# Attention and maxout FFN on one core: score matmuls of two pairs of heads gathered into three half-array stretches per turn, with raw inputs in four buffers

## The chip, the cores and the metric

One Trainium2 chip; the kernel runs on one core of it. The metric is the device time in microseconds (us) of one execution. The kernel before takes 367.87 us (median of three runs). TensorE is called PE here, as in the profile (its weight loads PEld), VectorE DVE, ScalarE ACT, GpSimd POOL, and SyncE, which issues most transfers, SP.

## The reference

Softmax attention with a one added to the denominator, over 8 batches of 12 heads, 448 positions and 64 features a head, and behind it a feed-forward layer with three up projections, their maximum, and one down projection:

```python
def _attn_ref(q, k, v):                       # each 8 x 12 x 448 x 64
    scores = scale * np.matmul(q, k.transpose(0, 1, 3, 2))
    m = np.max(scores, axis=-1, keepdims=True)
    e = np.exp(scores - m)
    attn = e / (np.sum(e, axis=-1, keepdims=True) + np.exp(-m) + 1e-09)
    return np.matmul(attn, v).astype(np.float32)
...
x = np.ascontiguousarray(attn_out.transpose(0, 2, 1, 3)).reshape(B * S, H * D)
def _moe_ref(x, w1, w2, w3, w_out):           # 3584 x 768, weights 768 x 768
    h = np.maximum(np.maximum(x @ w1, x @ w2), x @ w3)
    return (h @ w_out).astype(np.float32)
```

The kernel leaves the maximum out, so its softmax is exp(s) / (1 + sum of exp(s)), which is the same number.

## The kernel before

**Pairs.** Two heads make a pair, six pairs a batch, 48 pairs in all. The 448 keys of a head are three blocks of 128 and one of 64; the last blocks of both heads of a pair are put into one block of 128, the "last rows".

**Attention of a pair.** `scores(p, c)` (L239) computes block c for both heads: two matmuls that contract over 64 features, one on the upper and one on the lower 64 rows of the array. These run side by side, and such a pair of matmuls is called a half-array pair here. `scores_last(p)` (L255) is one full matmul for the last rows. ACT takes the exponents from PSUM into `eT` (`exp_scores`, L249, both heads in one instruction of 896 elements) and `eL` (`exp_last`, L265). `av_main(p, hh)` (L273) multiplies them with v in three full matmuls for a head; v has columns of ones beside it, so that the sums of the exponents come out on the other 64 partitions. `av_last(p)` (L285) adds the last rows: one half-array pair. `reciprocals` (L298, L299) makes 1 / (1 + sum) by a logarithm for each head and one exponent on ACT. `normalize(p, hh)` (L307) multiplies on DVE and writes half of `xT` for one pair.

**Feed-forward.** When a batch's six pairs are normalized, `batch_done` puts 18 up groups (six matmuls over 448 tokens each, L356, closed by a DVE instruction, L370 or L372) and 6 or 8 output groups (six matmuls over 384 columns, L390, closed by L415, and two output transfers for every second one, L429) on a Python list. `group()` takes the next one from it. So the order on every engine is written out by hand: between the steps of one pair's attention stand groups of the batch before.

**The loop.** One turn of the loop (L452) handles pair `it` and finishes pair `it - 1`. From batch 2 on (`it` of 12 and up, `P_DMA`) a turn is: `cast_qk(it + 2)` on DVE, `transposes(it + 2)` as one transposing transfer on SP (L209), `scale_v(it + 1)` on POOL (L157); scores 0 and 1 with their exponents; a group; `av_main` of the pair before; `av_last` of the pair before, scores 2, `scores_last`; the reciprocals and the other exponents on ACT; a group; normalize head 0; a group; normalize head 1; the remaining one or two groups; the loads of pair `it + 5` (six transfers on SP). There are thus two places a turn where the array works in halves: scores 0 and 1 (two half-array pairs), and `av_last` with scores 2 (two half-array pairs). In batches 0 and 1 the transposes are done by PE. Batch 0 has no feed-forward work yet, and idle matmuls (`keep_busy`) stand in its place.

**Buffers.** Scores lie in two PSUM buffers (`ps_s`), attention results in two (`ps_av`), groups in two (`ps_u`). The transposed q and k have three buffers (`qkT`), the scaled v three (`vst`), the casts two (`qk16`). Raw q, k and v lie in three sets of buffers of three pairs each (`NRAW`, `HB`). When a turn begins a batch, four groups of the batch before last are still on the list (`LEFT`).

Of the kernel before, what the change touches and what calls it, by code (L numbers as in the profile page):

```python
# [10 lines left out]
FP32 = mybir.dt.float32  # L11
# [10 lines left out]
def kernel(  # L22
# [11 lines left out]
    nc = tc.nc  # L34
# [29 lines left out]
    small = ctx.enter_context(tc.tile_pool(name="small", bufs=2))  # L64
    xt_pool = ctx.enter_context(tc.tile_pool(name="xt", bufs=2))
    ht_pool = ctx.enter_context(tc.tile_pool(name="ht", bufs=2))
    out_pool = ctx.enter_context(tc.tile_pool(name="outp", bufs=3))

    ps_s = ctx.enter_context(tc.tile_pool(name="ps_s", bufs=2, space=bass.MemoryType.PSUM))
    ps_av = ctx.enter_context(tc.tile_pool(name="ps_av", bufs=2, space=bass.MemoryType.PSUM))  # L70
# [2 lines left out]
    ctx.enter_context(tc.manual_schedule())  # L73


    NRAW = 3
    HB = NPAIR // 2
    raw = [
        [cpool.tile([128, 2 * HB, NB + 1, D], FP32, name=f"{n}in{i}") for n in "qkv"]
        for i in range(NRAW)  # L80
# [2 lines left out]
    def load(p0, n_pairs, names="qkv", engs=(nc.sync, nc.sync)):  # L83
        b, j = divmod(p0, NPAIR)
        tiles = raw[(p0 // HB) % NRAW]
        h0 = 2 * (p0 % HB)
        for name, t, src in zip("qkv", tiles, (q, k, v)):
            if name not in names:
                continue
            rows = src[b, 2 * j : 2 * (j + n_pairs)].rearrange("h (p c) d -> p h c d", c=TP)  # L90
            hs = slice(h0, h0 + 2 * n_pairs)
            engs[0].dma_start(out=t[0:64, hs, 0 : NB + 1, :], in_=rows[:, :, 0 : NB + 1, :])
            engs[1].dma_start(out=t[64:128, hs, 0:NB, :], in_=rows[:, :, NB + 1 : TP, :])
# [5 lines left out]
    load(1, 1, "qk")  # L99
    load(0, 1, "v")  # L100
    load(2, 1, "qk")
    load(1, 2, "v")
    load(3, 1, "qk")
    load(4, 2, "q")
    load(3, 1, "v")
    load(4, 2, "k")
    load(4, 2, "v")

    idle = cpool.tile([128, S], MMDT, name="idle")
    nc.vector.memset(idle, 0.0)  # L110
    for i in range(NRAW - 1):
        nc.vector.memset(raw[i][0][64:128, :, NB, :], 0.0)
    nc.vector.memset(raw[2][0][64:128, 0:2, NB, :], 0.0)
    load(NPAIR, 1, "qk")

    ident16 = cpool.tile([128, 128], MMDT, name="ident16")
# [44 lines left out]
    def casts(p):  # L161
        cast_qk(p)
        scale_v(p)

    def cast_qk(p):
        qt, kt, _ = raw[(p // HB) % NRAW]
        h0 = 2 * (p % HB)
        hs = slice(h0, h0 + 2)
        k6, q6 = k16[p % NK], q16[p % NK]
        if p == 0:  # L170

            nc.scalar.copy(out=k6[:, 0:NB], in_=kt[:, hs, 0:NB].rearrange("p h c d -> p c h d"))
            for eng, cs in ((nc.scalar.copy, slice(0, 2)), (nc.vector.tensor_copy, slice(2, NB + 1))):
                eng(out=q6[:, cs], in_=qt[:, hs, cs].rearrange("p h c d -> p c h d"))
        else:
            if p >= P_DMA and (p // NPAIR) % 2:

                nc.vector.tensor_copy(
                    out=q6[:, 1 : NB + 1], in_=qt[:, hs, 0:NB].rearrange("p h c d -> p c h d")
                )  # L180
                nc.vector.tensor_copy(out=q6[64:128, 0], in_=qt[0:64, hs, NB])
            else:
                nc.vector.tensor_copy(out=q6, in_=qt[:, hs].rearrange("p h c d -> p c h d"))  # L183
            nc.vector.tensor_copy(  # L184
                out=k6[:, 0:NB], in_=kt[:, hs, 0:NB].rearrange("p h c d -> p c h d")
            )
        for hh, half in enumerate(halves):
            last = nc.gpsimd if p == 0 else nc.vector
            last.tensor_copy(out=k6[half, NB, hh], in_=kt[0:64, h0 + hh, NB])  # L189

    def scale_v(p):
        vt = raw[(p // HB) % NRAW][2]
# [58 lines left out]
    def scores_last(p):  # L251

        stl = ps_s.tile([128, 2, 512], FP32, tag="s", name="stl")
        qkT, q0, k0 = qkTs.pop(p)
        nc.tensor.matmul(  # L255
            out=stl[:, 0, 0:S],
            lhsT=qkT[:, k0 + NB * 128 : k0 + NB * 128 + 128],
            rhs=qkT[:, q0 : q0 + S],
            start=True,
            stop=True,  # L260
        )
        return stl

    def exp_last(p, stl):
        nc.scalar.activation(out=eL[:, p % 2], in_=stl[:, 0, 0:S], func=AF.Exp, scale=scale)  # L265
# [183 lines left out]
    casts(0)  # L449
    transposes(0)  # L450
    keep_busy(3)
    for it in range(NP + 1):  # L452
        p = it if it < NP else None
        prev = it - 1 if it > 0 else None
        to_next = NPAIR - it % NPAIR
        n_groups = -(-max(len(queue) - LEFT, 0) // to_next) if it % NPAIR else 4
        n_groups = max(3, min(5, n_groups))

        first = {3: 1, 4: 2}.get(it)
        if first is not None:  # L460
            hs = slice(2 * first, 2 * first + 2)
            nc.vector.memset(raw[2][0][64:128, hs, NB - 1 : NB + 1, :], 0.0)
            if first == 1:
                load(NPAIR, 1, "v")
            load(NPAIR + first, 1)
        if it in (3, 4):
            load_weight(0, it - 3)
        if it in (5, 6, 8):
            load_weight((5, 6, 8).index(it) + 1)
        if it < NPAIR:  # L470

            casts(it + 1)
            for c in range(2):
                exp_scores(p, c, scores(p, c))
            if prev is None:
                keep_busy(3)
                exp_scores(p, 2, scores(p, 2))
                transposes(1)
                exp_last(p, scores_last(p))
            else:  # L480
                den, av = (ps_av.tile([128, 512], FP32, tag="av", name=n) for n in ("den", "av"))
                sums_main(prev, den, 1)
                stp = scores(p, 2)
                sums_main(prev, av, 0)
                stl = scores_last(p)
                sums_last(prev, den, 1)
                sums_last(prev, av, 0)
                exp_scores(p, 2, stp)
                exp_last(p, stl)
                rb = reciprocals_one(den)  # L490
                transposes(it + 1)
            if it < NPAIR - 1:
                keep_busy(3)
            else:

                ups = [up_open()]
                up_part(ups[0], 0, 0, 0, range(3))
                av5 = ps_s.tile([128, 2, 512], FP32, tag="s", name="av5")
                sums_main(p, av5[:, 1], 1)
                sums_main(p, av5[:, 0], 0)  # L500
                sums_last(p, av5[:, 1], 1)
                sums_last(p, av5[:, 0], 0)
                rb5 = reciprocals_one(av5[:, 1])
            if prev is not None:
                normalize_one(prev, av, rb)
            if it == NPAIR - 1:
                normalize_one(p, av5[:, 0], rb5)
                batch_done(0)
        elif it == NPAIR:
            exp_scores(p, 0, scores(p, 0))  # L510

            up_part(ups[0], 0, 0, 0, (3,))
            ups.append(up_open())
# [12 lines left out]
            exp_scores(p, 2, scores(p, 2))  # L526
            exp_last(p, scores_last(p))
            group()
            transposes(it + 1)
            group()  # L530
        else:
            late = it + 1 < P_DMA
            if not late:

                if it + 2 < NP:
                    cast_qk(it + 2)
                    transposes(it + 2)
                if it + 1 < NP:
                    scale_v(it + 1)
            if p is not None:  # L540
                for c in range(2):
                    exp_scores(p, c, scores(p, c))
            group()
            if late:
                casts(it + 1)
            avs = [av_main(prev, hh) for hh in range(2)]
            av_last(prev, avs)
            if p is not None:
                stp = scores(p, 2)
                stl = scores_last(p)  # L550
            rb = reciprocals(prev, avs)
            if p is not None:
                exp_scores(p, 2, stp)
                exp_last(p, stl)
            if late:
                transposes(it + 1)
            group()
            normalize(prev, 0, avs, rb)
            group()
            normalize(prev, 1, avs, rb)  # L560
            if it % NPAIR == 0:
                batch_done(prev // NPAIR)
# [6 lines left out]
        for n in range(NPAIR + HB, 2 * NPAIR) if it == NPAIR else (it + 5,):  # L569
            if it >= NPAIR and n < NP:  # L570
                load(n, 1)
    while queue:
        group()

# [29 lines left out]
```

## Time and profile before

| | |
|---|---|
| three runs | 367.97, 367.87, 367.87 us; median 367.87 |
| profiled execution: time / span | 367.07 / 365.3 us |
| granted TensorE clock over the span | 0.999 |
| busy: PE / PEld / DVE / ACT / POOL | 357.4 / 163.9 / 243.4 / 221.1 / 53.6 us |
| moved by transfers | 58.61 MB |

The span is the part of the profiled execution between its first and its last instruction; 1.8 us lie outside it. Busy times are unions of the instructions of an engine. Matmuls overlap in the array, so what a matmul costs is read from the start of one to the start of the next and not from its own duration.

### The profile page before, as it was taken

Reading aid. Unit: us, or ns where it says so; the run is one execution under the profiler, and the core shown is the slowest. Engines: PE = TensorE matmul, PEld = TensorE weight load, DVE = VectorE, ACT = ScalarE, POOL = GpSimd, SP = SyncE. Lnnn points to the kernel's source line nnn. Section 1 sums busy time; section 2 is a strip of 40 time slices with the busy share of each in tenths; the row PEclk is TensorE's granted clock in tenths of the full one; section 3 lists DMA queues with packets and bytes.
Section 4 is the critical chain, followed back from the end, with each engine's and each line's share of the span. In section 5 each row is a group of like instructions: output and inputs, shape, how many; then the busy total and the mean of one; then the engine's idle time right before and its main releaser. Section 6 shows DMA issues by size and latency. Waiting matters only on the chain.

```text
span 365.3 us, 6122 instructions
## 1 busy us (share of the span) xinstructions
PE 357.4 (98%) x2086; PEld 163.9 (45%) x2086; DVE 243.4 (67%) x521; ACT 221.1 (61%) x335; POOL 53.6 (15%) x159
## 2 busy tenths in 40 slices
PE   8999999999999999999999999999999999999995
PEld 3434444444444444444444444444444444445552
DVE  4474777876578677577657867757666776555553
ACT  4996476765666766666567666666566766651000
POOL 4263112211211211211121121121112112000000
PEclk9999999999999999999999999999999999999999
DMA  5999997668667888849764896758675673005006
GB/s 151 229 234 229 233 247 211 155 177 214 161 180 182 208 184 154 195 107 185 182 173 122 178 200 164 175 133 214 159 174 137 165 208 83 5 2 131 2 0 172
DMA packets 87951, 58.61 MB, mean 160 GB/s; under 512 B 43504, under 2 KB 84464, under 8 KB 87920
## 3 DMA queue, kind: packets, MB, share of 16 engines
q1 hardware_dynamic: 83632, 53.18, 59.7%
q0 software_dynamic: 3920, 4.72, 7.5%
q10 hardware_dynamic: 368, 0.33, 0.4%
q8 instruction: 16, 0.26, 0.3%
q14 instruction: 15, 0.12, 0.1%
HBM read 42.47 MB, written 11.01 MB: 146 GB/s over the span
## 4 chain that ended last, share of the span: by engine, by line
PE 91%; ACT 2%; DMA 2%; DVE 2%; issue 1%; SPq 0%; DVEq 0%
PE up L356 44%; PE op L390 15%; PE av L273 13%; PE stp L239 8%; PE stl L255 4%; PE av L285 3%; DMA kin<-in_k_dram 2%; PE busy L349 2%; ACT eT L249 1%; PE trT L221 1%; PE trT L226 1%; PE av L316 1%; DVE qkT L233 1%; DVE o_sb L415 0%; DVE qk L183 0%
## 5 line engine op out<-in xcount | busy, mean ns | idle before, releaser
L356 PE MATMUL up<-xT,w 128*128 128x448 f16 x864 | 175.3, 353 | 0.7 <-DVE xT L307 0.4
L249 ACT ACTIVATE eT<-stp 128x896 f16<-128x896 f32 x144 | 125.5, 910 | 53.3 <-PE stp L239 53.3
L356 PEld LDWEIGHTS <-w 128*128 128x128 f16 x864 | 81.7, 98 | 81.7 <-issue 12.5
L372 DVE TENSOR_TENSOR hT<-hT,up 128x448 f16<-128x448 f16 x96 | 59.6, 621 | 52.1 <-PE up L356 51.1
L157 POOL TENSOR_SCALAR vst<-vin 128x384 f16<-128x384 f32 x132 | 43.1, 338 | 255.2 <-issue 159.2
L298 ACT ACTIVATE lnd<-av 64x448 f32<-64x448 f32 x84 | 45.3, 539 | 49.0 <-PE av L285 48.0
L390 PE MATMUL op<-w,hT 128*128 128x384 f16 x336 | 59.3, 326 | 0.0
L273 PE MATMUL av<-eT,vst 128*128 128x448 f16 x252 | 54.5, 352 | 0.0
L307 DVE TENSOR_TENSOR xT<-av,rb 64x448 f16<-64x448 f32 x84 | 51.8, 617 | 1.4
L239 PE MATMUL stp<-qkT 64*128 64x448 f16 x288 | 44.1, 353 | 1.5 <-DVE qkT L233 0.7
L370 DVE CAST hT<-up 128x448 f16<-128x448 f32 x48 | 29.8, 624 | 22.9 <-PE up L356 22.2
L415 DVE TENSOR_SCALAR o_sb<-op 128x384 f32<-128x384 f32 (+1 forms) x56 | 30.8, 550 | 20.0 <-PE op L390 19.0
L390 PEld LDWEIGHTS <-hT 128*128 128x128 f16 x336 | 31.6, 98 | 24.7 <-issue 4.0
L273 PEld LDWEIGHTS <-vst 128*128 128x128 f16 x252 | 24.7, 98 | 22.4
L184 DVE CAST qk<-kin 128x384 f16<-128x384 f32 x47 | 25.7, 548 | 1.1 <-DMA kin<-in_k_dram 0.7
L265 ACT ACTIVATE eL<-stl 128x448 f16<-128x448 f32 x48 | 25.9, 539 | 0.0
L299 ACT ACTIVATE rb<-lnd 128x448 f32<-128x448 f32 x42 | 24.2, 576 | 1.3
L239 PEld LDWEIGHTS <-qkT 64*128 64x128 f16 x288 | 11.0, 94 | 23.2 <-issue 16.5
L419 ACT ACTIVATE o_sb<-op 128x192 f32<-128x192 f32 x1 | 0.3, 331 | 30.2 <-DVE o_sb L415 30.2
L189 DVE CAST qk<-kin 64x64 f16<-64x64 f32 x94 | 17.5, 187 | 1.3
L255 PE MATMUL stl<-qkT 128*128 128x448 f16 x48 | 17.4, 362 | 0.0
L285 PE MATMUL av<-eL,vst 64*128 64x448 f16 x84 | 15.2, 359 | 0.0
(50 smaller groups left out, 117.7 us busy)
## 6 DMA issues: line engine op xcount, KB each, us to landing
out_dram<-o_sb SPq DMA_DIRECT2D x54, 192.0 KB, 2.8
qin<-in_q_dram SPq DMA_DIRECT2D x46, 128.0 KB, 3.0
kin<-in_k_dram SPq DMA_DIRECT2D x45, 128.0 KB, 2.9
vin<-in_v_dram SPq DMA_DIRECT2D x44, 128.0 KB, 2.9
kin<-in_k_dram SPq DMA_DIRECT2D x46, 96.0 KB, 2.7
qin<-in_q_dram SPq DMA_DIRECT2D x45, 96.0 KB, 2.7
vin<-in_v_dram SPq DMA_DIRECT2D x44, 96.0 KB, 2.8
w<-in_moe_w_dram POOLq DMA_DIRECT2D x2, 1152.0 KB, 17.1
```

The source lines that it names most:

```text
L157: nc.gpsimd.tensor_scalar(out=out, in0=in_, scalar1=LAMBDA, scalar2=1.0, op0=ALU.mult, op1=ALU.mult)
L239: nc.tensor.matmul(out=stp[:, hh, 0:S], lhsT=qkT[hh * D : hh * D + D, k0 + c * 128 : k0 + c * 128 + 128], rhs=qkT[hh * D : hh * D + D, q0 ...
L249: nc.scalar.activation(out=eT[:, p % 2, c], in_=stp[:, :, 0:S], func=AF.Exp, scale=scale)
L255: nc.tensor.matmul(out=stl[:, 0, 0:S], lhsT=qkT[:, k0 + NB * 128 : k0 + NB * 128 + 128], rhs=qkT[:, q0 : q0 + S], start=True, stop=True,)
L273: nc.tensor.matmul(out=av[:, 0:S], lhsT=vst[:, p % VB, hh * NB + c, (1 - hh) * D : (3 - hh) * D], rhs=eT[:, p % 2, c, hh, :], start=(c == ...
L298: nc.scalar.activation(out=lnd[mine], in_=avs[hh][other, 0:S], func=AF.Ln, bias=1.0)
L307: nc.vector.tensor_tensor(out=xTs[b][mine, j, :], in0=avs[hh][mine, 0:S], in1=rb[mine], op=ALU.mult)
L356: nc.tensor.matmul(out=ps[:, 0:S], lhsT=w_sb[i][:, dc, ts(fc, 128)], rhs=xTs[b][:, dc, :], start=(dc == 0), stop=(dc == NDC - 1),)
L370: nc.vector.tensor_copy(out=h, in_=ps[:, 0:S])
L372: nc.vector.tensor_tensor(out=h, in0=h, in1=ps[:, 0:S], op=ALU.max)
L390: nc.tensor.matmul(out=ps[:, 0:NW], lhsT=hTs[sb][:, fc, ts(t, 128)], rhs=wout_sb[:, fc, ts(nh, NW)], start=(fc == 0), stop=(fc == NFC - 1),)
L415: nc.vector.tensor_scalar(out=o_sb[:, cs], in0=src, scalar1=1.0 / LAMBDA, scalar2=None, op0=ALU.mult)
```

## The change

From pair 12 on the loop goes by two pairs a turn, `p` and `p + 1` (18 turns). A turn has three half-array stretches in place of the four of two old turns:

1. `av_last(p - 1)`, scores 0 and 1 of `p`: three half-array pairs;
2. scores 2 of `p`, scores 0 of `p + 1`: two;
3. `av_last(p)`, scores 1 and 2 of `p + 1`: three.

The last rows of both pairs are computed in two full matmuls one behind the other (`scores_last2`) between groups, with one exponent instruction for both (`exp_last2`). Eight to ten groups are spread over the turn: three behind stretch 1, one to three behind the last rows, one behind stretch 2, three behind stretch 3. `av_main` stands behind stretch 2's group for `p` and at the turn's end for `p + 1`; so the loop before ends, at pair 11, with `av_main(11)`. The casts and the transposing transfer for `p + 2` come behind the groups that follow the last rows, those for `p + 3` behind stretch 2's group.

The raw inputs lie in four sets of buffers of two pairs each. From pair 10 on one load brings two pairs (six transfers for two pairs, each twice as large). In batch 0 the v of pairs 2 and 3 comes by two transfers issued by GpSimd; other early loads are issued in a slightly different order. Output tiles have five buffers in place of three. The number of matmuls, casts, groups and closing instructions is unchanged; exponents of last rows are half as many and twice as wide from pair 12 on.

```diff
-    out_pool = ctx.enter_context(tc.tile_pool(name="outp", bufs=3))
+    out_pool = ctx.enter_context(tc.tile_pool(name="outp", bufs=5))
...
-    NRAW = 3
-    HB = NPAIR // 2
+    NRAW = 4
+    HB = 2
...
-    load(1, 2, "v")
+    load(1, 1, "v")
     load(3, 1, "qk")
-    load(4, 2, "q")
-    load(3, 1, "v")
-    load(4, 2, "k")
+    load(4, 2, "qk")
     load(4, 2, "v")
...
+    def scores_last2(p):
+        stl = ps_s.tile([128, 2, 512], FP32, tag="s", name="stl")
+        for n in range(2):
+            qkT, q0, k0 = qkTs[p + n]
+            nc.tensor.matmul(out=stl[:, n, 0:S],
+                lhsT=qkT[:, k0 + NB * 128 : k0 + NB * 128 + 128],
+                rhs=qkT[:, q0 : q0 + S], start=True, stop=True)
+        return stl
+
+    def exp_last2(stl):
+        nc.scalar.activation(out=eL, in_=stl[:, :, 0:S], func=AF.Exp, scale=scale)
...
-    for it in range(NP + 1):
+    for it in range(P_DMA):
...
+            if it == 0:
+                load(2, 2, "v", (nc.gpsimd, nc.gpsimd))
             casts(it + 1)
...
+        if it in (6, 7, 9):
+            load({6: 10, 7: 12, 9: 14}[it], 2)
+    avs = [av_main(P_DMA - 1, hh) for hh in range(2)]
+    for p in range(P_DMA, NP, 2):
+        more = p + 2 < NP
+        left = max(len(queue) - LEFT, 0)
+        to_next = (NPAIR - p % NPAIR) // 2
+        n_groups = 8 if p % NPAIR == 0 else max(8, min(10, -(-left // to_next)))
+        av_last(p - 1, avs)
+        stps = [scores(p, c) for c in range(2)]
+        rb = reciprocals(p - 1, avs)
+        for c in range(2):
+            exp_scores(p, c, stps[c])
+        group()
+        normalize(p - 1, 0, avs, rb)
+        group()
+        normalize(p - 1, 1, avs, rb)
+        if p % NPAIR == 0:
+            batch_done(p // NPAIR - 1)
+        group()
+        exp_last2(scores_last2(p))
+        if more:
+            cast_q(p + 2)
+        for _ in range(n_groups - 7):
+            group()
+        if more:
+            cast_k(p + 2)
+            transposes(p + 2)
+        scale_v(p + 1)
+        stps = [scores(p, 2), scores(p + 1, 0)]
+        exp_scores(p, 2, stps[0])
+        exp_scores(p + 1, 0, stps[1])
+        group()
+        if more:
+            cast_qk(p + 3)
+            transposes(p + 3)
+            scale_v(p + 2)
+        if p + 6 < NP:
+            load(p + 6, 2)
+        avs = [av_main(p, hh) for hh in range(2)]
+        av_last(p, avs)
+        stps = [scores(p + 1, c) for c in (1, 2)]
+        rb = reciprocals(p, avs)
+        for c in (1, 2):
+            exp_scores(p + 1, c, stps[c - 1])
+        group()
+        for hh in range(2):
+            normalize(p, hh, avs, rb)
+        group()
+        group()
+        avs = [av_main(p + 1, hh) for hh in range(2)]
+    av_last(NP - 1, avs)
+    rb = reciprocals(NP - 1, avs)
...
```

`cast_q`, `cast_k` and `cast_k_last` are `cast_qk` cut into its parts. Code that only the old loop needed is gone.

More of the change, by code (lines that the diff above doesn't have):

```diff
@@ L112 @@
         nc.vector.memset(raw[i][0][64:128, :, NB, :], 0.0)
-    nc.vector.memset(raw[2][0][64:128, 0:2, NB, :], 0.0)
+    nc.vector.memset(raw[NRAW - 1][0][64:128, 0:2, NB, :], 0.0)
     load(NPAIR, 1, "qk")
@@ L165, in cast_qk @@
     def cast_qk(p):
[L166 to L169, printed above, removed]
         if p == 0:
-            nc.scalar.copy(out=k6[:, 0:NB], in_=kt[:, hs, 0:NB].rearrange("p h c d -> p c h d"))
+            qt, kt, _ = raw[0]
+            nc.scalar.copy(
+                out=k16[0][:, 0:NB], in_=kt[:, 0:2, 0:NB].rearrange("p h c d -> p c h d")
+            )
             for eng, cs in ((nc.scalar.copy, slice(0, 2)), (nc.vector.tensor_copy, slice(2, NB + 1))):
-                eng(out=q6[:, cs], in_=qt[:, hs, cs].rearrange("p h c d -> p c h d"))
-        else:
[L176 to L183, printed above, removed]
+                eng(out=q16[0][:, cs], in_=qt[:, 0:2, cs].rearrange("p h c d -> p c h d"))
@@ L184, in cast_qk, with cast_q @@
+            cast_k_last(0, nc.gpsimd)
+        else:
+            cast_q(p)
+            cast_k(p)
+    def cast_q(p):
+        qt = raw[(p // HB) % NRAW][0]
+        hs = slice(2 * (p % HB), 2 * (p % HB) + 2)
+        q6 = q16[p % NK]
+        if p >= P_DMA and (p // NPAIR) % 2:
             nc.vector.tensor_copy(
-                out=k6[:, 0:NB], in_=kt[:, hs, 0:NB].rearrange("p h c d -> p c h d")
+                out=q6[:, 1 : NB + 1], in_=qt[:, hs, 0:NB].rearrange("p h c d -> p c h d")
             )
+            nc.vector.tensor_copy(out=q6[64:128, 0], in_=qt[0:64, hs, NB])
+        else:
+            nc.vector.tensor_copy(out=q6, in_=qt[:, hs].rearrange("p h c d -> p c h d"))
@@ L187, in cast_qk, with cast_k, cast_k_last @@
+    def cast_k(p):
+        kt = raw[(p // HB) % NRAW][1]
+        hs = slice(2 * (p % HB), 2 * (p % HB) + 2)
+        nc.vector.tensor_copy(
+            out=k16[p % NK][:, 0:NB], in_=kt[:, hs, 0:NB].rearrange("p h c d -> p c h d")
+        )
+        cast_k_last(p, nc.vector)
+    def cast_k_last(p, eng):
+        kt = raw[(p // HB) % NRAW][1]
         for hh, half in enumerate(halves):
-            last = nc.gpsimd if p == 0 else nc.vector
-            last.tensor_copy(out=k6[half, NB, hh], in_=kt[0:64, h0 + hh, NB])
+            eng.tensor_copy(out=k16[p % NK][half, NB, hh], in_=kt[0:64, 2 * (p % HB) + hh, NB])
@@ L262, in scores_last @@
         return stl
+    def scores_last2(p):
+        stl = ps_s.tile([128, 2, 512], FP32, tag="s", name="stl")
+        for n in range(2):
+            qkT, q0, k0 = qkTs[p + n]
+            nc.tensor.matmul(
+                out=stl[:, n, 0:S],
+                lhsT=qkT[:, k0 + NB * 128 : k0 + NB * 128 + 128],
+                rhs=qkT[:, q0 : q0 + S],
+                start=True,
+                stop=True,
+            )
+        return stl
+    def exp_last2(stl):
+        nc.scalar.activation(out=eL, in_=stl[:, :, 0:S], func=AF.Exp, scale=scale)
     def exp_last(p, stl):
@@ L451 @@
     keep_busy(3)
-    for it in range(NP + 1):
-        p = it if it < NP else None
+    for it in range(P_DMA):
+        p = it
         prev = it - 1 if it > 0 else None
@@ L457 @@
         n_groups = max(3, min(5, n_groups))
[L459 to L463, printed above, removed]
+        if it in (3, 4, 6):
+            p_new = {3: 7, 4: 8, 6: 9}[it]
+            hs = slice(2 * (p_new % HB), 2 * (p_new % HB) + 2)
+            q_new = raw[p_new // HB % NRAW][0]
+            nc.vector.memset(q_new[64:128, hs, NB - 1 : NB + 1, :], 0.0)
+            if it == 3:
                 load(NPAIR, 1, "v")
-            load(NPAIR + first, 1)
+            load(p_new, 1)
         if it in (3, 4):
@@ L533 @@
             if not late:
[L535 to L542, printed above, removed]
+                cast_qk(it + 2)
+                transposes(it + 2)
+                scale_v(it + 1)
+                load(it + 5, 2)
+            for c in range(2):
+                exp_scores(p, c, scores(p, c))
             group()
@@ L547 @@
             av_last(prev, avs)
-            if p is not None:
-                stp = scores(p, 2)
-                stl = scores_last(p)
+            stp = scores(p, 2)
+            stl = scores_last(p)
             rb = reciprocals(prev, avs)
-            if p is not None:
-                exp_scores(p, 2, stp)
-                exp_last(p, stl)
+            exp_scores(p, 2, stp)
+            exp_last(p, stl)
             if late:
@@ L567 @@
                 group()
-        for n in range(NPAIR + HB, 2 * NPAIR) if it == NPAIR else (it + 5,):
-            if it >= NPAIR and n < NP:
-                load(n, 1)
+        if it in (6, 7, 9):
[9 more added lines that the diff above has]
+        rb = reciprocals(p - 1, avs)
+        for c in range(2):
+            exp_scores(p, c, stps[c])
[39 more added lines that the diff above has]
+    rb = reciprocals(NP - 1, avs)
+    group()
+    normalize(NP - 1, 0, avs, rb)
+    group()
+    normalize(NP - 1, 1, avs, rb)
+    batch_done(B - 1)
     while queue:
```

2 lines of the change are left out of this document (removed).

## The prediction

> **What bounds the kernel now.** I read the busy times and the slices of the page first, then the busy times by stretches, then the timeline of PE in one steady turn.
>
> ```profile
> PE 357.4 (98%) x2086; PEld 163.9 (45%) x2086; DVE 243.4 (67%) x521; ACT 221.1 (61%) x335; POOL 53.6 (15%) x159
> PEclk9999999999999999999999999999999999999999
> 73.10:327.70 254.60, 254.16 (x1441) 114.91 (x1441) 177.44 (x377) 166.70 (x253) 32.26 (x102) 1.00 0.66 159
> ```
>
> The third row is the stretch from the first turn of batch 2 to the end of the last pair's turn: 254.60 us, of which PE is busy 254.16, at the full clock. Nobody else is near: DVE 177, ACT 167. So only what shortens PE's own stream of instructions can gain there, and every wait that the new order gives PE is lost in full. "Busy" says nothing of how well the array is used, though, so I read the distance from start to start:
>
> ```profile
> 339.73 13.22 PE L356 MATMUL up<-xT,w 128*128 128x448 f16 x69
> 352.78 8.04 PE L390 MATMUL op<-w,hT 128*128 128x384 f16 x48
> ...
> 207.22 0.55 PE L239 MATMUL stp<-qkT 64*128 64x448 f16 x4
> 207.71 1.31 PE L356 MATMUL up<-xT,w 128*128 128x448 f16 x6
> 208.85 1.30 PE L273 MATMUL av<-eT,vst 128*128 128x448 f16 x6
> 210.08 0.36 PE L285 MATMUL av<-eL,vst 64*128 64x448 f16 x2
> 210.28 0.35 PE L239 MATMUL stp<-qkT 64*128 64x448 f16 x2
> 210.57 0.36 PE L255 MATMUL stl<-qkT 128*128 128x448 f16 x1
> 210.77 3.57 PE L356 MATMUL up<-xT,w 128*128 128x448 f16 x18
> 214.27 0.55 PE L239 MATMUL stp<-qkT 64*128 64x448 f16 x4
> ```
>
> 69 full matmuls take 352.78 - 339.73 = 13.05 us, 0.189 each. Now the turn from 207.22 to 214.27, 7.05 us: it has 6 + 6 + 1 + 18 = 31 full matmuls, 5.86 us, and four half-array pairs. A half-array pair inside a stretch takes 0.20 (210.08 to 210.28), together 0.80. 7.05 - 5.86 - 0.80 = 0.39 us are left, and there are two stretches: **each stretch costs 0.195 us beyond its work.** Where: entering, the six av matmuls take 208.85 to 210.08, 1.23 in place of 1.13; leaving, the last half-array pair takes 0.29 (210.28 to 210.57) in place of 0.20. The Trainium skill, "TensorEngine Tiling (Array Packing)", Key Properties, says that changing the tiling mode drains the array. By the 128 cycles of drain in its page "TensorE: Matmul & The Clock Gate" (Step-by-step) I estimate 0.05 us a switch, 0.11 a stretch and 1.9 us for 18 stretches; the rows show 0.195, and they decide.
>
> **The change, part by part.**
>
> *Half-array stretches.* Old turns 12 to 47 have two each, 72; the 18 new turns have three, 54. `av_last` of pair 47 stands alone in both. Matmuls and half-array pairs are equally many. 18 stretches x 0.195 = **-3.5 us**. That a third half-array pair in a row also costs 0.20 no row shows, since the trace has at most two. Bounds: 0.20, the second pair's price; or 0.29, if its weights could not be loaded beside the pair before.
>
> ```profile
> 210.09 0.10 PEld L239 LDWEIGHTS <-qkT 64*128 64x128 f16 x2
> L249 ACT ACTIVATE eT<-stp 128x896 f16<-128x896 f32 x144 | 125.5, 910 | 53.3 <-PE stp L239 53.3
> L299 ACT ACTIVATE rb<-lnd 128x448 f32<-128x448 f32 x42 | 24.2, 576 | 1.3
> L307 DVE TENSOR_TENSOR xT<-av,rb 64x448 f16<-64x448 f32 x84 | 51.8, 617 | 1.4
> L372 DVE TENSOR_TENSOR hT<-hT,up 128x448 f16<-128x448 f16 x96 | 59.6, 621 | 52.1 <-PE up L356 51.1
> 201.30 1.15 PE L390 MATMUL op<-w,hT 128*128 128x384 f16 x6
> 202.29 1.30 PE L273 MATMUL av<-eT,vst 128*128 128x448 f16 x6
> 210.48 1.10 ACT L298 ACTIVATE lnd<-av 64x448 f32<-64x448 f32 x2 [1.13 <-PE av L285]
> ```
>
> The second pair's weights are loaded (210.09) while the first still streams, as with full matmuls one behind the other, so I take 0.20.
>
> *New waits of PE.* I walk one turn with eight up groups, stretch 1 at 0. Three half-array pairs with the exit end at 0.69; three groups of 6 x 0.189 at 4.1; the last rows, 2 x 0.189, at 4.5; a group at 5.6; stretch 2, behind its entry, goes from 5.7 to 6.2; a group and `av_main` to 8.45; stretch 3 from 8.55 to 9.25; three groups to 12.65; `av_main` to 13.8; the next stretch 1 is at 13.9. A hand-over between engines takes 0.04 (the av pair ends at 210.08 + 0.36, the logarithm starts at 210.48). What PE needs, and when it is there:
> - Second half-array pair of stretch 2, at 5.9: the score buffer of the last rows. Their second matmul starts at 4.3 and takes 0.36; their exponent has 896 elements, 0.91 as in L249; with two hand-overs the buffer is free at 5.65. Slack 0.25. In the turn that opens a batch the first four groups are output groups of 0.98 (202.29 - 201.30), and the slack is 0.1.
> - `av_main(p + 1)`, at 12.65: the attention buffers of p. The logarithms start at 8.55 + 0.40 and take 1.10, the exponent 0.58: the reciprocal is there at 10.65. DVE closes a group until 11.2 (0.62 from 10.55) and normalizes twice, 0.617 each: free at 11.8 and 12.4, needed at 12.65 and 13.2. Slack 0.8. Its third matmul, at 13.0, needs ACT's second exponent behind the reciprocal: 10.65 + 2 x 0.91 = 12.5. Slack 0.5, and 0.1 where output groups stand behind stretch 3.
> - Scores 0 and 1 at the next turn's start need exponents that ended at 11.6 and 12.5.
>
> All of it hides, some of it by little: 0 taken, and what I have wrong here counts 18 times. A lost cover costs as much as the chain is late, the second rival below.
>
> *Casts, transposing transfers, loads.* `transposes(p + 2)` moves behind four groups and waits for `cast_k(p + 2)`. Behind it on SP are queued the other transposing transfer, the loads and the output transfers of the turn, none due within the turn. The fourth group's last matmul ends at 5.75, DVE closes it by 6.45, then casts k, 0.55, and two small pieces, 0.19 each: 7.4.
>
> ```profile
> L184 DVE CAST qk<-kin 128x384 f16<-128x384 f32 x47 | 25.7, 548 | 1.1 <-DMA kin<-in_k_dram 0.7
> L189 DVE CAST qk<-kin 64x64 f16<-64x64 f32 x94 | 17.5, 187 | 1.3
> DMA to landing us min/median/max: 2.7/3.1/5.5
> 15.52 0.60 SPq L92 DMA_DIRECT2D kin<-in_k_dram  x1
> 207.07 1.26 SPq L209 DMA_TRANSPOSE qkT<-qk  x1
> 208.42 4.15 SPq L429 DMA_DIRECT2D out_dram<-o_sb  x4
> 216.74 1.26 SPq L209 DMA_TRANSPOSE qkT<-qk  x1
> ```
>
> The landing row is that of the transposing transfers: 10.5, at the worst 12.9, and stretch 1 of the next turn needs it at 13.9. `transposes(p + 3)` goes out by about 10 and is needed at 19.6. SP before had the other trouble: between two transposing transfers (207.07 and 216.74) it issued four output transfers and six loads. A load of two pairs takes no longer to issue than one of one (0.60, the 15.52 row), so two pairs cost SP six issues in place of twelve, about 3.7 us less; PE did not wait for SP, so this gains 0, but it speaks against SP as the next bound: 2 x 1.3 + 6 x 0.65 + at most 8 output transfers of 0.65 make 11.7 of 13.9 us. Raw data have two turns to land. The wider exponent, the fifth output buffer and POOL's scaling lie beside PE: 0.
>
> *Where the old loop meets the new one.*
>
> ```profile
> 72.47 0.60 DVE L307 TENSOR_TENSOR xT<-av,rb 64x448 f16<-64x448 f32 x1
> 73.10 0.80 PE L239 MATMUL stp<-qkT 64*128 64x448 f16 x4
> 73.74 0.63 DVE L307 TENSOR_TENSOR xT<-av,rb 64x448 f16<-64x448 f32 x1
> 73.83 1.15 PE L390 MATMUL op<-w,hT 128*128 128x384 f16 x6
> 78.69 1.11 PE L356 MATMUL up<-xT,w 128*128 128x448 f16 x5
> 80.17 0.35 PE L356 MATMUL up<-xT,w 128*128 128x448 f16 x1 [0.37 <-DVE xT L307]
> ```
>
> `av_main(11)` now follows the third group of turn 11 at once, about 72.96, and needs what pair 10's normalizations free: its first head waits until 73.1, its second, due at 73.7, until 74.4: +0.9. Two waits go: the scores at 73.10 took 0.73 to the next instruction in place of 0.49, and five matmuls at 78.69 took 1.48 in place of 0.95, since the new batch's first group came before its last normalization; in the new turn its last matmul comes 5.0 us behind the stretch (0.69, three output groups, the last rows, five matmuls), and that normalization has ended by 4.2 (the av pair's chain to 2.1, then two output closings and two multiplications). -0.8. Together **+0.1**.
>
> *Batch 0.* The v of pairs 2 and 3 goes to GpSimd's queue, behind the scaling of pair 0's v.
>
> ```profile
> 8.93 0.55 POOL L157 TENSOR_SCALAR vlast<-vin 64x64 f16<-64x64 f32 x2
> 19.67 1.01 POOL L147 DMA_DIRECT2D w<-in_moe_w_dram  x1
> 20.65 0.76 PE L316 MATMUL av<-eT,vst 128*64 128x448 f16 x6
> w<-in_moe_w_dram POOLq DMA_DIRECT2D x2, 1152.0 KB, 17.1
> w<-in_moe_w_dram POOLq DMA_DIRECT2D x2, 576.0 KB, 8.5
> ```
>
> It is issued from 9.5 to 11.5 (1.0 each). The two carry 448 KB together; by the nearest row of this queue, 576 KB in 8.5, they land by 19.0 from an issue at 10.5. Pair 2's v is used at 20.65 and scaled in 0.5 before: due at 20.1, slack 1.1, so 0; by the 1152 KB row it would be 7.5 late, once. What SP no longer issues brings later loads forward by 1.3 us, which gains 0.
>
> Sum: -3.5 + 0.1 = -3.4. The profiled execution took 367.07 (span 365.3 and 1.8 around it), which gives 363.7; the median of the runs is 0.8 higher, 367.87, so the forecast for the median is **364.5**, 0.9% faster.
>
> **The rivals.**
> - *A third half-array pair pays for its weights.* Two of a turn's three stretches have one: 36 x 0.10 (the weight load of the 210.09 row) = 3.6, which leaves 368.1, no change; partly exposed, between 364.5 and that. For it: no stretch of three is in the trace. Against: the second pair's load hides. 0.12, half of it at the far end.
> - *PE waits in stretch 2 for the exponent of the last rows, and the kernel is slower.* It decides from the point where the chain of 1.35 us (matmul, exponent, hand-overs) is 0.4 longer than I add it up: 12 turns x 0.15 and 6 x 0.3 is the 3.5 gained. At 0.5 longer it is 12 x 0.25 + 6 x 0.4 = 5.4: 369.9. For it: slacks of 0.25 and 0.1 from rows that round by 0.05, and the wide exponent frees its buffer later than the old one of 448. Against: ACT is idle when it comes. 0.11.
> - *The transposing transfer lands after its turn has begun*, in the shadow of a burst of larger loads: decides at 6.5 us from cast to landing, where the worst of 5.5 from issue is seen; 0.5 late in 14 turns is 7, so 368 to 372. 0.04.
> - *The v by GpSimd comes late.* POOL builds the descriptors while DVE casts. By the bound above, 364.5 + 7.5 = 372.0. Against: the weights on the same queue beside the same casts moved 576 KB in 8.5. 0.05. The Trainium skill, "SBUF — State Buffer", SBUF: two separate sides, speaks against this part of the change: a transfer issued by GpSimd starves for descriptors while DVE copies fp32 between parts of SBUF, and one of 0.62 us became 3.1. By that ratio, as an estimate, 4.6 us would become 23 and batch 0 about 13 us longer; no run here shows it yet.
>
> **How the numbers follow.** Forecast 0.68, rivals 0.12, 0.11, 0.04, 0.05. A measurement of this kernel tells about 0.2%, 0.7 us, from no change. Faster: 0.68 and half of the first rival, 0.74; same: its other half, 0.06; slower: the other three, 0.20. The forecast's own range is 363.6 to 365.4: below, 0.2 us for the rounding of 0.195 and 0.7 of the 0.9 that the seam may not cost; above, waits of 0.05 in each turn. The range reaches over the first rival: 363.6 to 368.1.
>
> **What would show it.** PE's starts in a steady turn: about 13.9 us for eight up groups, 0.20 between all pairs of a stretch and 0.29 behind the last; a third pair at 0.29 is the first rival. A gap ahead of the second pair of stretch 2 is the second; one ahead of `av_last` or scores 0 at a turn's start the third; av matmuls of batch 0 later than 20.65 the fourth. PE busy should fall by about 3 us, and its idle time should not grow. I am wrong if the batches 2 to 7 together do not become 3 us shorter, or if batch 0 becomes longer.

## The result and the profile after

The changed kernel takes **364.74 us** (median of five runs, 364.29 to 365.22) against 367.87 before: ratio 0.9911, 95% interval 0.9898 to 0.9925. In a second set of rounds it took 364.92, ratio 0.9924 (0.9911 to 0.9937). The forecast was 364.5. The profiled execution after took 365.22, span 363.4, which is the slowest of the five.

I divide both traces at the same pieces of work: at `av_last` of pair 10, in turn 11, and at the first up group of the last batch. The rows are the busy times by stretches, first of before, then of after, there with the busy times of the whole execution above them (each row: stretch, length, PE busy, then the other engines, the clock, and the share and rate of the transfers):

```profile
0.00:70.14 70.14, 67.18 (x448) 30.25 (x449) 44.24 (x106) 49.93 (x74) 20.34 (x54) 1.00 0.95 215
70.14:332.24 262.10, 261.63 (x1485) 118.59 (x1485) 182.57 (x389) 170.87 (x260) 33.28 (x105) 1.00 0.66 157
332.24:365.30 33.06, 28.58 (x157) 15.07 (x155) 16.63 (x28) 0.33 (x1) 0.00 (x0) 0.98 0.27 71
```

```profile
PE 353.9 (97%) x2086; PEld 167.0 (46%) x2086; DVE 244.0 (67%) x523; ACT 219.8 (60%) x317; POOL 55.7 (15%) x161
...
0.00:71.53 71.53, 67.50 (x448) 30.21 (x449) 44.38 (x108) 49.91 (x74) 21.96 (x56) 1.00 1.02 221
71.53:330.18 258.65, 257.94 (x1484) 121.76 (x1484) 183.66 (x390) 169.55 (x242) 33.73 (x105) 1.00 0.65 156
330.18:363.40 33.22, 28.46 (x156) 15.08 (x155) 15.94 (x27) 0.33 (x1) 0.00 (x0) 1.00 0.27 70
```

The stretch that the new loop makes became 262.10 - 258.65 = **3.45 us shorter**, where the prediction's sum says 3.4 (stretches and seam together). PE's busy time fell by 3.5 us. The first two batches became 1.39 us longer, of which the prediction has nothing, and the tail 0.16. Together that is the 1.9 us between the spans. Two of the signs that the prediction named went against it in this execution: PE's idle time grew, from 7.9 to 9.5 us, and batch 0 became 0.3 us longer. Most of that comes from its term for the loads, below.

One turn of the new loop, the timeline of PE after:

```profile
201.53 0.36 PE L314 MATMUL av<-eL,vst 64*128 64x448 f16 x2
201.72 0.54 PE L251 MATMUL stp<-qkT 64*128 64x448 f16 x4
202.20 3.10 PE L419 MATMUL op<-w,hT 128*128 128x384 f16 x18
205.13 0.54 PE L281 MATMUL stl<-qkT 128*128 128x448 f16 x2
205.51 1.14 PE L419 MATMUL op<-w,hT 128*128 128x384 f16 x6
206.58 0.55 PE L251 MATMUL stp<-qkT 64*128 64x448 f16 x4
207.07 1.31 PE L385 MATMUL up<-xT,w 128*128 128x448 f16 x6
208.21 1.30 PE L302 MATMUL av<-eT,vst 128*128 128x448 f16 x6
209.44 0.36 PE L314 MATMUL av<-eL,vst 64*128 64x448 f16 x2
209.64 0.54 PE L251 MATMUL stp<-qkT 64*128 64x448 f16 x4
210.12 3.58 PE L385 MATMUL up<-xT,w 128*128 128x448 f16 x18
213.53 1.30 PE L302 MATMUL av<-eT,vst 128*128 128x448 f16 x6
214.76 0.36 PE L314 MATMUL av<-eL,vst 64*128 64x448 f16 x2
```

No row has idle time ahead of it. A stretch of three half-array pairs goes from 201.53 to 202.20, 0.67 us (0.69 in the prediction's walk), one of two from 206.58 to 207.07, 0.49, as before: the third pair costs 0.18 to 0.20, and the prediction's first rival is out.

### The profile page after: what moved, and what is told of

It reads as the page before. It is cut to its first block, busy times and chain, and to the rows that moved or that the text cites. A ratio compares the mean times of both kernels' runs of the same rounds, so it can differ in the third digit from the quotient of the medians.

```text
span 363.4 us, 5911 instructions
## 1 busy us (share of the span) xinstructions
PE 353.9 (97%) x2086; PEld 167.0 (46%) x2086; DVE 244.0 (67%) x523; ACT 219.8 (60%) x317; POOL 55.7 (15%) x161
## 4 chain that ended last, share of the span: by engine, by line
PE 84%; DMA 8%; SPq 3%; DVE 2%; ACT 1%; issue 1%; DVEq 0%
PE up L385 42%; PE op L419 14%; PE av L302 12%; PE stp L251 7%; DMA kin<-in_k_dram 5%; PE av L314 3%; DMA qin<-in_q_dram 2%; PE stl L281 2%; SPq L92 2%; SPq L93 1%; PE av L345 1%; ACT eT L261 1%; DVE o_sb L444 1%; PE trT L238 1%; DVE qkT L245 1%
## 5 line engine op out<-in xcount | busy, mean ns | idle before, releaser
L261 ACT ACTIVATE eT<-stp 128x896 f16<-128x896 f32 x144 | 123.5, 909 | 24.0 <-PE stp L251 24.0
L385 PEld LDWEIGHTS <-w 128*128 128x128 f16 x864 | 80.5, 98 | 86.7 <-issue 17.4
L251 PE MATMUL stp<-qkT 64*128 64x448 f16 x288 | 40.8, 352 | 1.5 <-DVE qkT L245 0.7
L291 ACT ACTIVATE eL<-stl 128x896 f16<-128x896 f32 x18 | 16.5, 917 | 14.2 <-PE stl L281 14.2
L251 PEld LDWEIGHTS <-qkT 64*128 64x128 f16 x288 | 12.8, 94 | 19.2 <-issue 11.7
L201 DVE CAST qk<-kin 64x64 f16<-64x64 f32 x94 | 20.5, 218 | 1.2
L188 DVE CAST qk<-qin 128x512 f16<-128x512 f32 x29 | 12.5, 432 | 1.3 <-DMA qin<-in_q_dram 1.1
```

The source lines that it names most:

```text
L251: nc.tensor.matmul(out=stp[:, hh, 0:S], lhsT=qkT[hh * D : hh * D + D, k0 + c * 128 : k0 + c * 128 + 128], rhs=qkT[hh * D : hh * D + D, q0 ...
L261: nc.scalar.activation(out=eT[:, p % 2, c], in_=stp[:, :, 0:S], func=AF.Exp, scale=scale)
L385: nc.tensor.matmul(out=ps[:, 0:S], lhsT=w_sb[i][:, dc, ts(fc, 128)], rhs=xTs[b][:, dc, :], start=(dc == 0), stop=(dc == NDC - 1),)
```

## The experiments

All kernels are compared with the kernel before, run on the same chip beside them (its medians were 367.52 to 367.65 in these rounds).

**Stretches put back: 72 and 90 in place of 54.** Each edit only moves a group between two half-array pairs of a stretch.

```diff
-        stps = [scores(p, 2), scores(p + 1, 0)]
-        exp_scores(p, 2, stps[0])
-        exp_scores(p + 1, 0, stps[1])
-        group()
+        exp_scores(p, 2, scores(p, 2))
+        group()
+        exp_scores(p + 1, 0, scores(p + 1, 0))
```

> The changed kernel with stretch 2 taken apart: scores 2 of p, the group, then scores 0 of p + 1, so 72 stretches from pair 12 on in place of 54, with all else as changed. Theory (each stretch costs 0.195 us beyond its work): 18 x 0.195 = 3.5 us more than the changed kernel's 364.74, so 368.2, and 0.39 between the two pairs' surroundings in every turn. Rival (the gain comes from buffers, bigger loads and SP's relief, and the stretches cost nothing in sum): 364.7.

```diff
-        stps = [scores(p + 1, c) for c in (1, 2)]
+        stp = scores(p + 1, 1)
         rb = reciprocals(p, avs)
-        for c in (1, 2):
-            exp_scores(p + 1, c, stps[c - 1])
-        group()
+        exp_scores(p + 1, 1, stp)
+        group()
+        exp_scores(p + 1, 2, scores(p + 1, 2))
```

> Stretch 3 taken apart too: av_last and scores 1 of p + 1, a group, scores 2 of p + 1. 90 stretches. Theory: 36 x 0.195 = 7.0 us more than the changed kernel, 371.7, and equal steps from 54 to 72 to 90. Rival (three half-array pairs in a row are what helps or hurts, not the number of stretches): the second step differs from the first by more than 1 us. Rival of the buffers: 364.7.

Measured: 368.69 us (ratio 1.0025, 1.0015 to 1.0035) and 372.20 (1.0124, 1.0111 to 1.0137). The steps from the changed kernel's 364.74 are 3.95 and 3.51 us, for 3.5 each. The traces say the same without the start of the kernel: from `av_last` of pair 10 to that of pair 47 the three kernels take 254.13, 257.95 and 261.55 us, steps of 3.82 and 3.60. With 72 stretches the two-pair turn has the time of the old loop and 1 us more. The gain is the number of stretches. In the timeline of PE with 72 stretches, stretch 2 now stands in two:

```profile
208.13 0.36 PE L251 MATMUL stp<-qkT 64*128 64x448 f16 x2
208.43 1.31 PE L385 MATMUL up<-xT,w 128*128 128x448 f16 x6
209.67 0.36 PE L251 MATMUL stp<-qkT 64*128 64x448 f16 x2
209.96 1.31 PE L302 MATMUL av<-eT,vst 128*128 128x448 f16 x6
```

Six full matmuls take 1.24 ahead of a half-array pair (1.13 otherwise), and the lone pair 0.29.

**The old loop with the new buffers and loads.** The loop of before, with `NRAW = 4`, `HB = 2`, five output buffers, loads of two pairs and GpSimd's v.

> The loop of before, one pair a turn with its four stretches for two pairs, with the changed kernel's raw buffers, loads and output buffers. Theory (the loop gains 3.4, the loads lose at the start): 367.87 plus what the first two batches lose, 0.4 for pair 3's q and k in batch 0 and 1.0 for pair 10's k in batch 1 by the profile after, so 368.3 to 369.3. Rival (the loads and buffers bring the gain): 364.7 to 366.

Measured: 368.23 us, ratio 1.0014 (1.0005 to 1.0023). The buffers and loads by themselves gain nothing and cost 0.6 us, at the start: from `av_last` of pair 10 to that of pair 47 this kernel takes 258.82 us, as before, and ahead of that PE's transposes wait 1.2 us for pair 10's k, as in the changed one.

**The new loop with the old buffers and loads.** Three raw sets of three pairs, loads of one pair, and three output buffers; then the same with five output buffers.

```diff
-        if p + 6 < NP:
-            load(p + 6, 2)
+        for n in (p + 5, p + 6):
+            if n < NP:
+                load(n, 1)
```

> The loop by two pairs with three stretches, but with the raw buffers (three of three pairs), the single-pair loads, the early loads and the three output buffers of before. Theory (the gain is the loop's alone): 3.4 us less than the kernel before, and without the 1.0 that pair 10's k loses in the changed kernel, 363.5 to 364.2. Rival (SP needs the larger loads: 2 x 1.3 + 12 x 0.65 + up to 8 x 0.65 make 15.6 us in a turn of 13.9, and the transposing transfers come late): slower than the changed kernel, 366 or more.

> The loop by two pairs with the raw buffers and single-pair loads of before, but five output buffers in place of three. Theory (the three stalls of 4.6 us in the run with three output buffers are an output tile that waits for a buffer whose transfer stands behind twelve loads on SP; five buffers cover that): the stalls go, about 18 us less, 363.5 to 365.5. Rival (SP is over its capacity with twelve single loads a turn, and any number of buffers only shifts the stall): 370 or more, with waits for the transposing transfer at the turns' starts.

Measured: **386.82 us** (1.0522, 1.0490 to 1.0554) with three output buffers and **375.08** (1.0197, 1.0161 to 1.0233) with five. My theory fell in both runs, and the rival is right for the first turn of each batch, in which the batch's six or eight output transfers are issued: there SP cannot carry twelve single loads beside the rest. SP is not full in the other turns: over the whole kernel with five buffers it waits 33.8 us for DVE's casts. With three buffers, in such a first turn:

```profile
214.49 0.60 SPq L93 DMA_DIRECT2D vin<-in_v_dram  x1
215.19 6.90 SPq L460 DMA_DIRECT2D out_dram<-o_sb  x8
218.96 0.56 DVE L446 TENSOR_SCALAR o_sb<-op 128x384 f32<-128x384 f32 x1 [5.10 <-DMA out_dram<-o_sb]
219.57 2.29 PE L387 MATMUL up<-xT,w 128*128 128x448 f16 x6 [4.29 <-DVE o_sb L446]
```

The output transfers go out only when the last load has (214.49), DVE waits 5.10 for an output buffer that such a transfer still reads, and PE waits 4.29 behind DVE. This comes three times, in the turns with eight output transfers. With five buffers that wait is gone and the next thing behind the loads and outputs is late, the transposing transfer (the last row is the sum of PE's waits for it at stretch 1, with their number and the longest):

```profile
212.09 0.60 SPq L93 DMA_DIRECT2D vin<-in_v_dram  x1
212.80 5.59 SPq L460 DMA_DIRECT2D out_dram<-o_sb  x8
218.50 2.73 SPq L223 DMA_TRANSPOSE qkT<-qk  x2
222.32 0.55 PE L253 MATMUL stp<-qkT 64*128 64x448 f16 x4 [1.56 <-DMA qkT<-qk]
...
PE stp L253 <- DMA qkT<-qk: 6.5, 6, 2.2
```

The six waits lie behind the output transfers of the six batches. Both runs also have the old raw buffers and early loads; that the number of loads is what matters is read from SP's rows, and no run changes it alone. Nor does a run give the new loop the larger loads with three output buffers.

In the changed kernel the same rows read:

```profile
203.27 5.59 SPq L458 DMA_DIRECT2D out_dram<-o_sb  x8
208.97 3.89 SPq L221 DMA_TRANSPOSE qkT<-qk  x2
```

with the turn's stretch 1 at 201.53 and the next at 214.76: the transfer goes out 7.4 us into the turn and lands in time. The walk also had 7.4, from the end of DVE's cast, which is at 208.50 here. But the walk put the output transfers behind the transposing one, and SP issues all eight of them ahead of it, until 208.86. That the two times meet is luck.

**The v of pairs 2 and 3 by SP.** Behind q and k of pair 3, and then behind those of pairs 4 and 5.

```diff
     load(3, 1, "qk")
+    load(2, 2, "v")
     load(4, 2, "qk")
...
-            if it == 0:
-                load(2, 2, "v", (nc.gpsimd, nc.gpsimd))
```

> The changed kernel with the v of pairs 2 and 3 issued by SP behind q and k of pair 3, not by GpSimd before them. Theory (GpSimd's transfer shares the 16 engines with q and k of pair 3 and makes them 0.4 us late): PE's transposes of pair 3 no longer wait at 17.7 us, 0.4 us faster than the changed kernel in the same rounds, 364.3. Rival (q and k of pair 3 are late whatever carries v): no change.

```diff
     load(3, 1, "qk")
     load(4, 2, "qk")
+    load(2, 2, "v")
     load(4, 2, "v")
...
-            if it == 0:
-                load(2, 2, "v", (nc.gpsimd, nc.gpsimd))
```

> The changed kernel with the v of pairs 2 and 3 issued by SP behind q and k of pairs 4 and 5 in place of GpSimd. Theory (SP's six tenths of a us for each issue set when early loads arrive; whatever SP issues later comes too late in batch 0): k of pair 4 is in time again, v of pair 2 is issued at 15.5 and lands at about 21, where it is due at 20.1, so about 1 us slower than the changed kernel. Rival (only the order of k of pair 4 mattered): no change or 0.4 faster.

Measured: 366.48 us (0.9960, 0.9946 to 0.9974) and 367.87 (1.0004, 0.9994 to 1.0014), 1.7 and 3.0 slower than the changed kernel. In the first, the wait at 17.7 us is gone, as the theory says, but the gain of 0.4 does not come, since a longer wait follows a turn later, for k of pair 4 (DVE and PE of that kernel):

```profile
23.24 0.55 DVE L194 CAST qk<-kin 128x384 f16<-128x384 f32 x1 [2.38 <-DMA kin<-in_k_dram]
23.85 0.54 PE L239 MATMUL trT<-ident,qk 128*128 128x128 f16 x4 [1.90 <-DVE qk L194]
```

In the second, v of pair 2 is scaled at 23.28 and PE waits 3.3 us for it; its 1 us was too small, since v landed about 7 us after its issue and not 5.5:

```profile
23.28 0.51 POOL L156 TENSOR_SCALAR vst<-vin 128x384 f16<-128x384 f32 x1 [9.86 <-DMA vin<-in_v_dram]
23.84 0.76 PE L346 MATMUL av<-eT,vst 128*64 128x448 f16 x6 [3.27 <-POOL vst L156]
```

So two issues of 0.6 us more on SP cost 1.7 and 3.0 us in batch 0, and GpSimd's queue is worth that to these loads. Part of the cost is the clock, which falls to half behind these waits (last section): in the profile of the first run the turn from 25.14 to 30.73 takes 5.59 us, where the one from 14.32 to 18.62 took 4.30.

**Pairs 10 and 11 loaded singly.**

```diff
-        if it in (6, 7, 9):
-            load({6: 10, 7: 12, 9: 14}[it], 2)
+        if it == 6:
+            load(10, 1)
+            load(11, 1)
+        if it in (7, 9):
+            load({7: 12, 9: 14}[it], 2)
```

> The changed kernel, but pairs 10 and 11 are loaded one behind the other as before, not together. Theory (pair 10's k waited for pair 11's share of the same transfer): the wait of 1.0 us of PE's transposes at 58.8 goes, 1.0 us faster than the changed kernel, 363.7. Rival (the transfer engines are full until about 70 us with weights and raw data, so k of pair 10 is late however it is cut): less than 0.3 us.

**Both normalizations of pair 10 ahead of turn 11's third group.**

```diff
             normalize(prev, 0, avs, rb)
-            group()
-            normalize(prev, 1, avs, rb)
+            if it + 1 == P_DMA:
+                normalize(prev, 1, avs, rb)
+                group()
+            else:
+                group()
+                normalize(prev, 1, avs, rb)
```

> The changed kernel, but in turn 11 both normalizations of pair 10 stand ahead of the third group. Theory (av_main(11) waits 0.9 us for the second normalization, which stands behind a closing instruction of 0.56): 0.6 us faster than the changed kernel, 364.1. Rival (another engine sets the end of that wait): no change.

Measured: 363.36 us (0.9883, 0.9870 to 0.9896) and 363.85 (0.9893, 0.9880 to 0.9905): 1.4 and 0.9 less than the changed kernel by the medians, 1.0 and 0.7 by the ratios to the kernel before, which is about what the waits come to. The waits in the changed kernel (PE and DVE), then the same places in the two kernels:

```profile
58.60 0.39 PE L233 MATMUL trT<-ident,qk 128*128 128x128 f16 x4
59.12 0.55 DVE L193 CAST qk<-kin 128x384 f16<-128x384 f32 x1 [1.27 <-DMA kin<-in_k_dram]
59.73 0.54 PE L238 MATMUL trT<-ident,qk 128*128 128x128 f16 x4 [0.74 <-DVE qk L193]
...
74.52 0.73 PE L302 MATMUL av<-eT,vst 128*128 128x448 f16 x3
75.13 0.63 DVE L336 TENSOR_TENSOR xT<-av,rb 64x448 f16<-64x448 f32 x1
75.82 0.74 PE L302 MATMUL av<-eT,vst 128*128 128x448 f16 x3 [0.57 <-DVE xT L336]
```

```profile
58.26 0.39 PE L233 MATMUL trT<-ident,qk 128*128 128x128 f16 x4
58.48 0.39 PE L238 MATMUL trT<-ident,qk 128*128 128x128 f16 x4
```

```profile
73.90 1.40 PE L302 MATMUL av<-eT,vst 128*128 128x448 f16 x6
```

Four transposes take 0.22 where they took 1.13, and the six av matmuls run through.

**Sums.** First the three early edits together, with v by SP behind pair 3:

> The changed kernel with v of pairs 2 and 3 by SP, pairs 10 and 11 loaded singly, and the normalizations of pair 10 ahead of the third group. Theory: the three sum up, 364.74 - 0.4 - 1.0 - 0.6 = 362.7. Rival (what one wait loses the next one absorbs): 363.7 to 364.3.

Measured 364.59 us (0.9926, 0.9906 to 0.9946), above both expectations. The v by SP, which costs 1.7 alone, takes back what the other two gain. Then those two without it, beside the changed kernel once more:

> The changed kernel with two edits: pairs 10 and 11 loaded one behind the other, and both normalizations of pair 10 ahead of turn 11's third group. The v of pairs 2 and 3 stays with GpSimd. Theory (the two waits lie one behind the other on PE and nothing absorbs them): the changed kernel less 1.0 and 0.6, 1.6 us faster than it in the same rounds, 363.1 or a little under. Rival (the second is absorbed by the first): 0.9 to 1.1 faster.

> The changed kernel once more, beside these three. Theory: 364.3 to 365.2, as before, with the wait for pair 10's k at 58 us in its profile and the one for pair 3's q and k at 17.7 there in some executions only.

Measured: **362.95 us**, ratio 0.9868 (0.9856 to 0.9881), against 364.92 for the changed kernel in the same rounds. This is the fastest version, 2.0 us under the changed kernel; the two waits do add up.

## Why the prediction was right, step by step

- **Price of a stretch.** 0.195 us by the rows of before. The runs with 54, 72 and 90 stretches give steps of 3.95 and 3.51 for 18, so 0.20 to 0.22 each, and 0.20 to 0.21 by the traces. Where it lies was right too: 0.10 on entering and 0.09 on leaving, also for a lone half-array pair. The Trainium skill, "TensorEngine Tiling (Array Packing)", Key Properties, names the drain, and the rows agree that a change of mode costs; the 0.11 that I had estimated from the 128 cycles of the Trainium skill, "TensorE: Matmul & The Clock Gate", Step-by-step, is half of what the runs show.
- **Third half-array pair.** Taken at 0.20, measured 0.18 to 0.20 (201.72 to 202.20 holds two pairs and an exit of 0.09).
- **New waits, 0.** Right. A turn of eight up groups takes 13.88 us (131.38 to 145.26), where the walk had 13.9. The tightest chain, in a turn that opens a batch, was to have a slack of 0.1:

```profile
205.71 0.92 ACT L291 ACTIVATE eL<-stl 128x896 f16<-128x896 f32 x1 [0.47 <-PE stl L281]
206.99 1.73 ACT L261 ACTIVATE eT<-stp 128x896 f16<-128x896 f32 x2 [0.36 <-PE stp L251]
```

  The exponent of the last rows ends at 206.63; the second half-array pair of stretch 2 starts at 206.58 + 0.20 = 206.78 and does not wait. ACT was idle on both sides, and with 0.15 us to spare the second rival did not come.
- **Seam, +0.1.** The waits came as walked: 0.16 and 0.73 us where I had 0.9 (the rows at 74.52 and 75.82), and the old waits of 0.8 are gone. The run that reorders the normalizations gains 0.9 by the medians and 0.6 in its trace (253.50 us from `av_last` of pair 10 to that of pair 47, for 254.13).
- **Loads, 0.** This term was mis-sized: it is about 1 us, at two places. In six traces with these early loads `av_last` of pair 10 starts at 70.90 to 71.53, where it started at 70.14 before. I gave raw data two turns to land, which is so from batch 2 on; pairs 10 and 11, loaded while the transfer engines still carry weights, were not walked. One transfer for both pairs brings pair 10's k later than one of its own: this costs PE 1.1 us in the profiled execution, 0.5 in the second profile of this kernel, and nothing when they are loaded singly (`av_last` of pair 10 at 70.12). And in batch 0, where I also had 0, q and k of pair 3 are late:

```profile
17.49 0.39 PE L233 MATMUL trT<-ident,qk 128*128 128x128 f16 x4
18.01 0.54 PE L238 MATMUL trT<-ident,qk 128*128 128x128 f16 x4
```

  The second row comes 0.3 us late, with 0.2 more inside it; this shows in three profiles with the same early code and not in others, among them that of the singly loaded pairs. That GpSimd's transfer, which now runs ahead of q and k of pair 3, makes them late is argued and not shown: the run that takes it away has no such wait, but some runs with it have none either. These two, less 0.1 that was gained ahead of them, are the 1.39 us of the first stretch. That the forecast still fits is in part luck. Between the two profiled executions only 1.9 us lie, where 3.4 were forecast; but that of before is faster than the runs around it by 0.8, and that of after is the slowest of its five. By the medians the gain is 3.1 us, and 2.7 in the second set of rounds. Where the other executions of before spend their 0.8 us no trace shows.
- **SP relief and fifth output buffer, 0.** Right as numbers of this change, and incomplete as working: I did not ask what the new loop would cost without them, and I had the order of SP's queue wrong in the first turn of a batch, where the outputs go ahead of the transposing transfer. The sum that I made for SP (11.7 of 13.9 us, and that turn is only 13.2 long) becomes 15.6 with single loads, and the two runs show what that means, 10 to 22 us. The old loop has no use for the relief (368.23); the new one, with the raw buffers and loads of before, loses more than it gains. So the parts of this change do not add: the loop with the old loads +7.6 with five output buffers and +19 with three, the loads and buffers alone +0.6, all together -3.1.
- **The v by GpSimd.** Its two transfers landed 4.6 and 5.2 us after their issue, under the 8.5 that I took, and v of pair 2 was scaled at 16.1, due at 20.1. The Trainium skill, "SBUF — State Buffer", SBUF: two separate sides, says that a GpSimd transfer is held up while DVE copies fp32 within SBUF, but until that copy ends and not in proportion, so the prediction's 23 us by its ratio was a wrong use of it. Whether DVE's casts here are such copies no run shows; these two transfers took little longer than SP's loads of two pairs of v before (4.6), and both runs that give them back to SP are slower.

## What to carry to other kernels

Where TensorE is the bound and has no gaps, read its stream from start to start and count its changes between half and full array: 0.2 us each way and back here, gained by putting half-array work side by side as far as the score buffers allow. Then walk each queue, above all the one that issues the transfers, for the new order as it would be without the rest of the change: a part that gains nothing alone may be what the gain stands on. Walk the first and the last turns separately; the steady turn was right to 0.05 us, and nearly all of the error lay in the start.

## What the runs showed of the hardware that I had not expected

A wait of PE can cost more than its length. After the wait of 4.29 us in the run with three output buffers, and after one of 2.24 in the run with five, the granted clock was half for the next 3 us (busy times by stretches of the two kernels; the clock is the third column from the right). The third row is from the run with v behind pair 3's q and k, after its wait of 1.90 us:

```profile
219.50:223.00 3.50, 3.43 (x10) 1.46 (x10) 3.18 (x10) 0.00 (x0) 0.00 (x0) 0.53 0.60 175
```

```profile
135.20:138.20 3.00, 2.90 (x10) 1.02 (x11) 0.00 (x0) 1.73 (x2) 0.00 (x0) 0.50 0.74 185
```

```profile
24.20:29.00 4.80, 4.62 (x24) 1.32 (x25) 2.98 (x7) 2.64 (x3) 3.47 (x8) 0.64 1.17 250
```

Six up matmuls took 2.29 us in the first of these in place of 1.31. In the third the clock is still full when the wait ends at 23.85; it is half from about 25.4 to 28.6, while PE is busy. So the drop need not follow the wait at once. The Trainium skill, "TensorE: Matmul & The Clock Gate", Part 1, describes this gate with a window of about 3.4 us that runs free of the kernel; the way back to full speed agrees, while idle times of 2.24 and 1.90 us were already enough here. The wait of 1.56 us in the run with five buffers left the clock full in the 3 us behind it, and the waits under 1 us of the changed kernel leave it at 1.000.
